# A new order table for a decayed linear attention and a feed-forward layer on one core

## The chip, the core and the metric

The kernel runs on one core of a Trainium2 chip. A core has TensorE (PE; its weight loads are shown as PEld), VectorE (DVE), ScalarE (ACT), GpSimd (POOL) and SyncE (SP), which here only issues transfers, and sixteen DMA engines that all queues share. The metric is device time of one launch in microseconds (us). Before the change it is 187.21 us, the median of three runs (187.03 to 187.23). Profiles come from one further execution of the same program.

## The reference

There are 4 batches, 8 heads, 768 steps and 48 channels a head. First a recurrence with a complex decay, then a layer norm and a feed-forward layer with a residual:

```python
mag = np.sqrt(a_re * a_re + a_im * a_im)
scale = np.minimum(mag, 0.999) / (mag + 1e-06)
...
for t in range(S):
    new_re = ar * S_re - ai * S_im
    new_im = ar * S_im + ai * S_re
    kv = np.einsum('bhd,bhe->bhde', k[:, :, t], v[:, :, t])
    S_re, S_im = (new_re + kv, new_im)
    y[:, :, t] = np.einsum('bhd,bhde->bhe', q[:, :, t], S_re)
...
xn = (x - mu) / np.sqrt(var + 1e-06) * g_ln
ch = np.maximum(xn @ w_ch1, 0.0) @ w_ch2
return (x + ch).astype(np.float32)
```

The output is 4 x 768 x 384 in float32; w_ch1 is 384 x 1536, w_ch2 is 1536 x 384.

## The kernel before

The 768 steps of a batch are cut into chunks of 128 steps, two chunks make a pair, three pairs a batch; so pairs P run from 0 to 11 and chunks n from 0 to 23, with n = 2P + c. The running product of the decays is replaced by cumulative sums of logarithms and of angles, made by matmuls with triangular matrices.

For a pair: loads of are, aim, k, q, vf (v as float32) on SP; `ln`, `iv`, `th`, `u` on ScalarE and `r`, `r2`, `l`, `lc` on VectorE or GpSimd turn a_re and a_im into log magnitude and angle; `dec` and `ph` are the matmuls that sum these; `e` and `en` are the decay and its inverse, `sin` and `cos` the rotation. The decay products are `ke` = k * en and `qe` = q * e, two halves a pair (`ke.P.0.m`), and `ks`, `qs` multiply these by cos and sin (`.0` is cos, `.1` sin). Pair 0 is worked in two halves of four heads, so there the third part of a name is always one of these halves (`qs.0.0.0`: half 0, cos).

For a chunk: `kT`, `qT` transpose ks and qs on TensorE (line 598), `ksT`, `qsT` copy the result out of PSUM; or, where the table gives `ksT` or `qsT` to SP, a transfer that transposes does both, and kT or qT is left out (line 603). `am` multiplies the two (line 621), `atm` masks, `gm` is the sum of k and v products (line 645) that `G` carries on, `y` the attention's output (lines 682 and 685). `v` is vf as bfloat16 (lines 408 and 410). Then `bn` and `x` for the norm, `xtr` and `xT` the transpose of x (line 719; or a transfer, line 725), `mm1` and `relu` (lines 752, 764, 766), `mm2` (line 776), `ot` (line 791) and the store `st` (line 797). `xr` and `rstd` finish the norm behind the matmuls.

The weights come by two transfers on GpSimd's queue: `wl.0` (line 365) and `wl.1` (line 367). They land as bfloat16. `ngl` (line 373) is the negated norm gain, and `wc` (line 381, VectorE) scales the first weights by it in nine pieces. All of `mm1` needs these.

Nothing is scheduled by a planner at run time. `PLAN` (line 42) is a table in which each word is an operation, its engine (P, A, V, G, S) and, for what uses PSUM, its first bank; a name behind "@" is an operation on another engine after which this one may start ("turns at the shared port"). Each engine runs its words in the order of the table, and waits for what an operation needs, for its tile's buffer (`RINGS`: three of q and k, two of vf, ten of x) and for its bank. SP sends its transfers in order too. `warm` are matmuls on a constant that fill TensorE (lines 806 and 810); `tab` loads ScalarE's function tables (line 815).

Of the kernel before, what the change touches and what calls it, by code (L numbers as in the profile page):

```python
# [846 lines left out]
```

## Time and profile before

| | before |
|---|---|
| median of three runs | 187.21 us |
| the profiled execution, span from first to last instruction | 185.6 us |
| TensorE, VectorE, ScalarE, GpSimd busy | 177.0, 157.7, 154.6, 99.8 us |
| transfers on SP's queue | 127616 packets, 32.65 MB |
| of these, transposes: ksT, qsT, xT | 8, 7, 4 |
| read from and written to device memory | 28.31 MB, 4.72 MB |

The profiled execution is known by its span alone; launch and end lie outside it. A group row of the profile gives line, engine, operation, what is written and read, shape and count, then busy time and the mean duration of one in ns, then the engine's idle time ahead of these instructions and what ended most of it. Matmuls overlap, so their mean duration is longer than the pace at which they follow each other; the pace is read from the chain of waits.

### The profile page before, as it was taken

To read this page: it belongs to the slowest core of one execution; us is meant where nothing else is said; L and a number is where in the kernel's file an instruction comes from. 1 tells how busy PE (TensorE), PEld (TensorE's weight loads), DVE (VectorE), ACT (ScalarE), POOL (GpSimd) and SP (SyncE) were. 2 spreads that over 40 slices of the span, in tenths; PEclk is the share of its full clock that TensorE was granted. 3 is DMA by queue.
4 is the path that set the end of the run, shared out by engine and by line. 5 is a ranking of instruction groups with operands and counts; after the bars stand their busy time and mean duration, and the time that the engine had idled before them with its cause. 6 is when DMAs were issued, how large, how long until landed. Compare 5 with 4: busy or idle time off the path is not lost.

```text
span 185.6 us, 5131 instructions
## 1 busy us (share of the span) xinstructions
PE 177.0 (95%) x2029; PEld 139.0 (75%) x2029; DVE 157.7 (85%) x302; ACT 154.6 (83%) x218; POOL 99.8 (54%) x128
## 2 busy tenths in 40 slices
...
GB/s 154 309 229 206 246 199 191 206 143 189 262 187 213 226 228 230 212 273 181 222 238 151 168 150 241 190 227 200 183 159 139 246 147 202 163 193 73 70 82 87
DMA packets 128440, 35.34 MB, mean 190 GB/s; under 512 B 124448, under 2 KB 127648, under 8 KB 128416
## 3 DMA queue, kind: packets, MB, share of 16 engines
q1 hardware_dynamic: 127616, 32.65, 81.4%
q0 software_dynamic: 800, 2.36, 7.2%
...
HBM read 28.31 MB, written 4.72 MB: 178 GB/s over the span
## 4 chain that ended last, share of the span: by engine, by line
PE 59%; ACT 14%; DMA 10%; DVE 10%; issue 3%; SPq 2%; DVEq 0%
PE banks L752 22%; PE banks L776 19%; DMA w1b<-in_moe_w_ch_dram 7%; PE banks L598 4%; PE banks L621 4%; ACT L815 3%; PE banks L484 2%; DMA are<-in_a_re_dram 2%; DMA k<-in_k_dram 2%; ACT are L457 2%; PE banks L682 2%; DVE l L473 1%; ACT h L764 1%; PE banks L685 1%; ACT w L455 1%
## 5 line engine op out<-in xcount | busy, mean ns | idle before, releaser
L752 PE MATMUL banks<-xT,w1b 128*128 128x256 bf16 x432 | 52.7, 273 | 0.2
L776 PE MATMUL banks<-w2b,h 128*128 128x384 bf16 (+2 forms) x300 | 52.5, 319 | 0.0
L752 PEld LDWEIGHTS <-w1b 128*128 128x128 bf16 x432 | 45.8, 114 | 1.7 <-DVE w1b L381 0.4
L764 ACT ACTIVATE h<-banks 128x1024 bf16<-128x1024 f32 x33 | 32.8, 1022 | 8.3 <-PE banks L752 8.1
L776 PEld LDWEIGHTS <-h 128*128 128x128 bf16 x300 | 26.9, 97 | 14.1
L292 DVE TENSOR_TENSOR atm<-banks,mask 128x1024 bf16<-128x1024 f32 x24 | 28.9, 1218 | 1.9 <-PE banks L621 1.6
L815 ACT ACT_TABLE_LOAD x15 | 19.2, 1283 | 1.0 <-PEq L831 0.8
L292 POOL TENSOR_TENSOR ke<-k,en 128x384 bf16<-128x384 f32 x14 | 12.7, 916 | 8.3 <-DVE l L476 5.6
L292 POOL TENSOR_TENSOR qe<-q,e 128x384 bf16<-128x384 f32 x15 | 13.7, 916 | 6.1 <-DVE w1b L381 1.9
L292 POOL TENSOR_TENSOR ks<-ke,trig 128x768 bf16<-128x768 bf16 x7 | 11.4, 1643 | 6.4 <-PE banks L752 4.2
L621 PE MATMUL banks<-qsT,ksT 128*128 128x128 bf16 x192 | 14.6, 219 | 0.1
L410 POOL TENSOR_SCALAR v<-vf 128x768 bf16<-128x768 f32 x7 | 5.8, 831 | 16.0 <-DVE r L292 8.9
L810 PE MATMUL banks<-u_e 128*128 128x512 f16 x42 | 11.7, 418 | 2.2 <-POOL u_e L320 2.2
L292 POOL TENSOR_TENSOR r<-aim,are 128x768 f16<-128x768 f32 x7 | 12.7, 1817 | 1.9 <-ACT x L699 1.5
L709 POOL TENSOR_SCALAR xr<-x,mv 128x384 f32<-128x384 bf16 x16 | 9.3, 586 | 8.1 <-PE banks L752 3.3
L621 PEld LDWEIGHTS <-ksT 128*128 128x128 bf16 x192 | 12.0, 98 | 1.8 <-DVE ksT L289 0.5
L692 DVE BATCH_NORM_STATS2 stats<-banks 128x6 f32<-128x384 f32 x24 | 13.4, 556 | 0.1
L682 PE MATMUL banks<-v,atm 128*128 128x48 bf16 x192 | 12.1, 183 | 0.3 <-ACT x L699 0.2
L473 DVE SCALAR_TENSOR_TENSOR l<-r,w 128x768 f16<-128x768 f16 (+1 forms) x13 | 11.5, 892 | 0.9 <-ACT r L469 0.7
L791 DVE SCALAR_TENSOR_TENSOR ot<-banks,rstd,xr 128x384 f32<-128x384 f32 (+2 forms) x18 | 10.5, 590 | 2.0 <-PE banks L776 1.6
L455 ACT ACTIVATE w<-are 128x768 f32<-128x768 f32 (+1 forms) x13 | 10.2, 790 | 2.3 <-DMA are<-in_a_re_dram 2.3
L682 PEld LDWEIGHTS <-atm 128*128 128x128 bf16 x192 | 11.0, 96 | 1.2 <-DVE atm L292 0.2
...
## 6 DMA issues: line engine op xcount, KB each, us to landing
k<-in_k_dram SPq DMA_DIRECT2D x24, 192.0 KB, 4.1
q<-in_q_dram SPq DMA_DIRECT2D x24, 192.0 KB, 4.2
vf<-in_v_dram SPq DMA_DIRECT2D x24, 192.0 KB, 4.0
out_dram<-ot SPq DMA_DIRECT2D x23, 192.0 KB, 3.4
are<-in_a_re_dram SPq DMA_DIRECT2D x8, 384.0 KB, 4.7
aim<-in_a_im_dram SPq DMA_DIRECT2D x8, 384.0 KB, 4.8
are<-in_a_re_dram SPq DMA_DIRECT2D x8, 192.0 KB, 3.7
aim<-in_a_im_dram SPq DMA_DIRECT2D x8, 192.0 KB, 3.8
```

The lines of the kernel that those rows point to most:

```text
L292: {"DVE": nc.vector, "POOL": nc.gpsimd}[eng(name)].tensor_tensor(**kw)
L455: add(f"ln.{X}", lambda S_=S_: act(out=S_("w"), in_=S_("are"), func=AF.Ln), needs=[f"are.{X}"], uses=[("are", P), ("w", P)])
L473: nc.vector.scalar_tensor_tensor(out=S_("l"), in0=S_("r2"), scalar=0.5, in1=S_("w"), op0=ALU.mult, op1=ALU.add)
L621: nc.tensor.matmul(ps[:, h], lhsT=T("ksT", n)[:, h], rhs=T("qsT", n)[:, h], start=True, stop=True)
L682: nc.tensor.matmul(ps[:, h], lhsT=T("atm", n)[:, h], rhs=T("v", P)[:, c, h], start=True, stop=nfirst)
L692: nc.vector.bn_stats(out=T("stats", n), in_=bank(f"y.{n}")[:, 0:DM])
L752: nc.tensor.matmul(ps[:, jj], lhsT=w1b[:, dc, ts(gi, JG * C)].rearrange("k (p j) -> k j p", j=JG)[:, jj], rhs=T("xT", P)[:, dc].rearrange( ...
L764: act(out=dst, in_=src, func=AF.Relu)
L776: nc.tensor.matmul(bank(f"o.{N}")[:, ws], lhsT=T("h", P)[:, j, ts(c, C)], rhs=w2b[:, j, ws], start=(j == 0), stop=(j == NJ - 1))
L791: nc.vector.scalar_tensor_tensor(out=o, in0=bank(f"o.{N}")[:, ws], scalar=T("rstd", P)[:, ds(c, 1)], in1=xs, op0=ALU.mult, op1=ALU.add)
L810: g.add(f"warm.w{i}", lambda i=i: nc.tensor.matmul(bank(f"warm.w{i}"), lhsT=u_e[:, 0, 0], rhs=u_e.rearrange("p c j t -> p (c j t)"), start ...
L815: g.add(f"tab.{nm}.{i}", lambda tab=tab: nc.scalar.preload_act_table_set(tab))
```

## The change

Only the table is new. It holds the same operations but for the transposes that go from TensorE to the transfer queue, and one evacuation.

- Eight more transposes are transfers: qsT.11, ksT.13, qsT.14, ksT.16, qsT.19, qsT.21 (six of ks or qs), xT.10 and xT.23. With them kT.13, kT.16, qT.11, qT.14, qT.19, qT.21, xtr.10 and xtr.23 leave TensorE.
- From VectorE to GpSimd: ten of the half products ke and qe in balance (GpSimd 14 and 15 before, 19 and 20 after), two r, two r2, two v, one G; in balance one ks, one qs, one xr and one ot go the other way.
- Between ScalarE and VectorE: x is 9 on ScalarE and 15 on VectorE before, 16 and 8 after; relu 33 and 3 before, 29 and 7 after; abs 6 and 2 before, 3 and 5 after.
- The order changes on all engines, the first loads included. On GpSimd the words between wl.0 and wl.1 were ke.1.0.0, ke.1.0.1, ks.1.0.1, ks.1.0.0, one, r.3.0, v.1, xr.0, ngl, r2.3.0; now they are ke.1.0.1, v.0, ke.1.0.0, ks.1.0.0, r.3.0, v.1, r2.3.0, one, ke.2.0.0, ngl.

The start of the table, up to the first mm1, before and after, and from the rest the lines with a new transposing transfer:

```diff
@@ -40,105 +40,104 @@
-are.1.0:S ue:G are.0.0:S are.0.1:S pad.qs.1:G pad.ks.2:G aim.1.0:S ident:G car0.0:G pad.qs.2:G aim.0.0:S tab.log.0:A
-ln.1.0:A uec:G aim.0.1:S qrow:G iv.1.0:A uth:V are.2.0:S zdec:G@uth ln.0.0:A car0.1:G@uth ln.0.1:A pick:G@uth iv.0.1:A
-k.0.0:S pad.qs.0:G iv.0.0:A q.0.1:S r.1.0:V q.0.0:S r.0.1:V tab.trig.1:A th.1.0:A r.0.0:V r2.0.1:V th.0.1:A r2.1.0:V
-vf.0.1:S th.0.0:A r2.0.0:V warm.w0:P0 warm.w1:P0 warm.w2:P0 warm.w3:P0 warm.w4:P0 warm.w5:P0 warm.w6:P0 warm.w7:P0
-warm.w8:P0 warm.w9:P0 warm.w10:P0 warm.w11:P0 warm.w12:P0 warm.w13:P0 warm.w14:P0 warm.w15:P0 warm.w16:P0 warm.w17:P0
-warm.w18:P0 warm.w19:P0 warm.w20:P0 warm.w21:P0 warm.w22:P0 warm.w23:P0 warm.w24:P0 warm.0:P0 warm.1:P0 warm.2:P0
-ph.0.1:P0 pad.ks.0:G@r2.0.0 aim.2.0:S ph.0.0:P6 car.0.1:V0 mask:G@r2.0.0 car.0.0:V6 pad.ks.1:G@r2.0.0 k.0.1:S
-warm.w25:P1 warm.3:P1 warm.4:P1 ph.1.0:P2 tab.log.2:A u.0.1:A u.0.0:A l.0.1:V k.1.1:S u.1.0:A l.0.0:V lc.0.1:V
-ln.2.0:A car.1.0:V2 q.1.1:S warm.w26:P1 warm.w27:P1 warm.5:P1 warm.6:P1 dec.0.1:P1 lc.0.0:V l.1.0:V en.0.1:A1
-warm.7:P4 dec.0.0:P7 e.0.1:A1 iv.2.0:A q.1.0:S lc.1.0:V qe.0.1.0:V warm.w28:P4 warm.w29:P4 warm.8:P4 warm.9:P4
-warm.10:P4 dec.1.0:P4 en.0.0:A7 uthc:V vf.0.0:S e.0.0:A7 r.2.0:V e.1.0:A4 warm.11:P1 warm.12:P1 dps.0:P7 are.3.0:S
-r2.2.0:V en.1.0:A4 ke.0.0.0:V u.2.0:A gln:S ke.0.1.0:V qe.0.0.0:V aim.3.0:S qe.1.0.1:V qe.1.0.0:V k.1.0:S l.2.0:V
-tab.trig.3:A sin.0.0:A6 sin.0.1:A0 warm.w30:P1 warm.w31:P1 warm.w32:P1 warm.w33:P1 warm.13:P1 warm.14:P1@en.1.0
-warm.w34:P1 warm.w35:P1 warm.w36:P1 warm.w37:P1 warm.15:P1 warm.16:P1@qe.0.0.0 warm.w38:P1 warm.w39:P1 warm.w40:P1
-warm.17:P1 warm.18:P1 warm.19:P1 warm.20:P1 qt.0.0:P6 qs.0.0.1:V sin.1.0:A2 qt.0.1:P0 ks.0.0.1:V vf.1.1:S lc.2.0:V
-cos.0.0:A6 ks.0.1.1:V warm.21:P1 warm.22:P1 qt.1.0:P2 qs.1.0.1:V cos.0.1:A0 vf.1.0:S dps.1:P5 qs.0.1.1:V cos.1.0:A2
-dec.2.0:P0 ks.0.1.0:V k.2.1:S ks.0.0.0:V decc.0:A7 qs.0.1.0:V kT.0:P6 decc.1:A5 qs.0.0.0:V th.2.0:A qs.1.0.0:V
-wl.0:G@qs.0.0.0 qT.0:P2 q.2.1:S v.0:V qT.1:P3 ksT.0:A6 qsT.0:V2 qT.2:P4 ke.1.0.0:G@v.0 k.2.0:S kT.1:P5 qsT.1:A3
-qsT.2:V4 am.0:P6 ke.1.0.1:G@v.0 ksT.1:V5 gm.0:P4 atm.0:V6 ks.1.0.1:G warm.23:P2 warm.24:P2 am.1:P2 qT.3:P5 tab.log.4:A
-ln.3.0:A atm.1:V2 y.0:P6 ks.1.0.0:G G.0:A4 e.2.0:A0 warm.w41:P7 warm.25:P7 warm.26:P7 warm.27:P7 gm.1:P4 bn.0:V6
-ph.2.0:P2 iv.3.0:A qsT.3:V5 one:G kT.2:P7 x.0:A6 G.1:V4 r.3.0:G en.2.0:A0 ksT.2:V7 warm.28:P5 xtr.0:P6 kT.3:P4 xT.0:V6
-am.2:P0 ksT.3:V4 y.1:P5 v.1:G atm.2:V0 am.3:P6 tab.trig.5:A th.3.0:A xr.0:G gm.2:P4 bn.1:V5 ngl:G sin.2.0:A2 r2.3.0:G
-ph.3.0:P0 atm.3:V6 x.1:A5 q.2.0:S car.3.0:A0 y.2:P5 G.2:V4 sin.3.0:A0 xtr.1:P7 qt.2.0:P2 are.4.0:S wc.1.1:V gm.3:P4
-xT.1:A7 wc.1.0:V qt.3.0:P0 wc.1.2:V cos.2.0:A2 wl.1:G@xT.1 vf.2.0:S wc.0.0:V mm1.0.1.0:P6 wc.0.1:V cos.3.0:A0 bn.2:V5
+ue:G are.0.1:S are.1.0:S are.0.0:S uth:V aim.1.0:S warm.13:P5 pad.qs.1:G warm.w5:P5 warm.w40:P5 aim.0.0:S ident:G
+warm.w17:P1 warm.7:P3 warm.0:P4 warm.w41:P2 aim.0.1:S uec:G warm.27:P3 tab.log.0:A ln.0.1:A warm.w24:P0 warm.w29:P2
+pick:G@uth are.2.0:S warm.w33:P4 iv.0.1:A warm.w25:P7 warm.6:P1 warm.w13:P3 warm.w22:P6 ln.1.0:A car0.1:G@uth
+warm.w14:P5 qrow:G warm.w11:P5 gln:S warm.18:P2 warm.w23:P1 ln.0.0:A zdec:G@uth q.0.1:S car0.0:G warm.w15:P6 iv.1.0:A
+warm.24:P3 warm.w3:P5 warm.25:P1 warm.8:P2 warm.26:P0 q.1.0:S warm.w19:P1 iv.0.0:A warm.20:P5 r.1.0:V warm.w27:P7
+warm.w16:P6 warm.w4:P1 warm.w26:P2 warm.w31:P7 k.0.0:S r.0.0:V warm.w10:P1 warm.w39:P5 r2.0.0:V warm.22:P1
+tab.trig.1:A th.1.0:A warm.10:P6 warm.12:P5 r.0.1:V warm.w21:P5 warm.w6:P7 k.0.1:S warm.w20:P4 th.0.0:A r2.0.1:V
+warm.4:P5 warm.w0:P2 th.0.1:A r2.1.0:G warm.5:P4 q.0.0:S ph.0.1:P1 warm.16:P4 warm.9:P4 aim.2.0:S ph.0.0:P0 car.0.1:V1
+pad.ks.0:G@r2.0.0 tab.log.2:A u.0.1:A warm.w8:P4 pad.qs.0:G warm.w30:P7 q.1.1:S u.0.0:A warm.w9:P6 l.0.1:V
+mask:G@r2.0.0 warm.w2:P4 u.1.0:A warm.11:P6 l.0.0:V pad.ks.1:G@r2.0.0 vf.0.1:S lc.0.1:V ln.2.0:A l.1.0:V dec.0.1:P4
+k.2.0:S en.0.1:A4 lc.0.0:V iv.2.0:A lc.1.0:V dec.0.0:P6 ke.0.1.0:V dec.1.0:P2 aim.3.0:S e.0.0:A6 car.0.0:V0 e.0.1:A4
+r.2.0:V k.1.0:S e.1.0:A2 warm.w7:P4 qe.0.1.0:V en.0.0:A6 vf.1.0:S r2.2.0:V en.1.0:A2 warm.w34:P6 ke.0.0.0:V are.3.0:S
+u.2.0:A qe.1.0.0:V ph.1.0:P2 qe.1.0.1:V l.2.0:V vf.0.0:S warm.w12:P6 dps.0:P7 warm.w35:P6 warm.14:P6@en.1.0 decc.0:V7
+k.1.1:S qe.0.0.0:G tab.trig.3:A sin.0.0:A0 car.1.0:V2 sin.0.1:A1 qt.0.0:P0 sin.1.0:A2 q.2.1:S qt.0.1:P1 lc.2.0:V
+ks.0.0.1:V qs.0.1.1:V cos.0.0:A0 qt.1.0:P2 qs.0.0.1:V cos.0.1:A1 ks.0.0.0:V vf.1.1:S warm.w18:P6 warm.28:P4 ks.0.1.1:V
+th.2.0:A warm.15:P6 warm.w28:P4 qs.0.0.0:V warm.w38:P6 qs.0.1.0:V q.2.0:S wl.0:G@qs.0.0.0 cos.1.0:A2 ks.0.1.0:V
+qT.0:P6 qs.1.0.1:V warm.19:P5 are.4.0:S warm.17:P1 qs.1.0.0:V kT.0:P4 qsT.0:V6 kT.1:P2 ke.1.0.1:G k.2.1:S qT.3:P0
+ksT.0:V4 tab.log.4:A ln.3.0:A qT.1:P5 v.0:G@qsT.0 ksT.1:V2 warm.3:P1 am.0:P6 qsT.1:A5 qsT.3:V0 ke.1.0.0:G qT.2:P3
+dps.1:P2 atm.0:V6 iv.3.0:A warm.21:P1 warm.w1:P4 ks.1.0.0:G@qsT.3 am.1:P0 decc.1:A2 warm.w36:P5 aim.4.0:S qsT.2:A3
+atm.1:V0 warm.2:P2 gm.0:P2 dec.2.0:P4 G.0:A2 ks.1.0.1:V en.2.0:A4 y.0:P0 gm.1:P2 uthc:V bn.0:V0 kT.2:P3 r.3.0:G@uthc
+e.2.0:A4 kT.3:P6 ksT.2:V3 x.0:A0 y.1:P4 G.1:V2 xtr.0:P5 am.2:P0 ksT.3:V6 v.1:G warm.w37:P2 ph.2.0:P2 atm.2:V0 r2.3.0:G
+tab.trig.5:A th.3.0:A am.3:P6 xT.0:A5 bn.1:V4 ph.3.0:P0 sin.2.0:A2 one:G ke.2.0.0:G atm.3:V6 vf.2.0:S x.1:A4 y.2:P5
+ngl:G@bn.1 sin.3.0:A0 wl.1:G wc.1.2:V xtr.1:P7 wc.1.1:V qt.2.0:P2 car.3.0:A0 wc.1.0:V gm.2:P4 xT.1:A7 q.4.1:S
+pad.ks.2:G wc.0.0:V qt.3.0:P0 G.2:V4 cos.2.0:A2 qe.2.0.0:G warm.1:P6 mm1.0.1.0:P6 bn.2:V5 vf.2.1:S cos.3.0:A0
...
...
+qsT.11:S G.8:V7 dec.6.0:P4 car.6.0:A0 abs.6.0:V0 k.5.0:S am.8:P2 r2.7.0:G e.6.0:A4 vf.5.0:S mm2.6.0:P6 atm.8:V2
...
+mm2.9.1:P1 x.10:A0 qe.6.0.1:G gm.10:P2 iv.9.0:A ph.8.0:P4 G.10:V2 xT.10:S qs.6.0.0:V mm2.8.0:P2 ks.6.0.1:V y.11:P3
+qs.6.0.1:V ksT.13:S mm2.9.2:P1 tab.trig.11:A sin.8.0:A4 bn.11:V3 r.9.0:G@qs.6.0.1 kT.12:P7 abs.8.0:A4 x.11:V3
...
+en.8.0:A2 qsT.14:S y.12:P6 mm2.10.1:P1 r.10.0:G bn.12:V6 x.13:A4 mm2.10.2:P1 e.8.0:A2 qsT.15:S x.12:V6 xtr.13:P7
...
+qs.8.0.0:V en.10.0:A6 ksT.16:S mm2.12.0:P3 ot.13:V1 qs.8.0.1:G@ks.8.0.0 bn.15:V0 mm2.12.1:P3 st.13:S xtr.14:P2 x.15:V0
...
+ke.9.0.0:V gm.16:P2 qsT.18:S y.16:P3 G.16:V2 relu.7.1:A0 ks.9.0.1:G ph.11.0:P4 bn.16:V3 qsT.19:S am.17:P6 cos.10.0:A
...
+G.19:V7 x.19:A5 xT.18:S mm2.16.0:P6 qs.10.0.0:V en.11.0:A2 qs.10.0.1:V mm2.16.1:P6 e.11.0:A2 xr.17:V qsT.21:S
...
+xr.19:G mm1.10.2.1:P4 xT.22:S ot.19:G@x.22 mm2.20.1:P6 relu.10.2:A4 mm2.21.0:P2 xT.23:S mm2.20.2:P6 mm2.21.1:P2
...
```

141 lines of the change are left out of this document (66 added, 75 removed).

## The prediction

> **What bounds the kernel now.** I read the page's first part, then the busy time by stretches, cut where the first matmul of the expert layer (mm1.0, line 752) starts and at later stage borders. The columns are PE, PEld, DVE, ACT, POOL busy, granted clock, DMA share, GB/s.
>
> ```profile
> span 185.6 us, 5131 instructions
> PE 177.0 (95%) x2029; PEld 139.0 (75%) x2029; DVE 157.7 (85%) x302; ACT 154.6 (83%) x218; POOL 99.8 (54%) x128
> 0.00:37.48 37.48, 32.63 (x317) 20.01 (x318) 28.70 (x58) 33.90 (x53) 18.74 (x40) 1.00 0.99 216
> 37.48:104.48 67.00, 66.96 (x796) 54.73 (x797) 63.88 (x125) 64.95 (x89) 37.45 (x41) 1.00 0.98 209
> 104.48:130.86 26.38, 26.27 (x324) 21.48 (x321) 24.94 (x49) 25.23 (x36) 17.53 (x19) 1.00 0.97 202
> 130.86:164.71 33.85, 33.82 (x425) 28.22 (x422) 29.65 (x58) 25.46 (x37) 20.64 (x22) 1.00 0.90 173
> 164.71:182.02 17.31, 17.30 (x178) 14.55 (x175) 10.13 (x16) 5.04 (x6) 5.40 (x9) 1.00 0.33 94
> ```
>
> From 37.48 us to 182.02 us TensorE is never idle (144.4 of 144.5 us) at full clock. ScalarE and VectorE stand just below it until 104 us (64.95 and 63.88 of 67.00), and the DMA engines are filled until 131 us. So the time has three terms: the start of mm1.0, the TensorE work behind it, and 3.6 us of last output and store behind 182.02. The first two are what this change touches.
>
> The chain of waits (start, length, what) gives TensorE's pace and what stood ahead of mm1.0:
>
> ```profile
> 24.53 12.18 DMA w1b<-in_moe_w_ch_dram
> 37.48 0.89 PE banks L752 x6
> 46.53 0.89 PE banks L598 x16
> 74.69 0.33 PE banks L719 x6
> 143.22 0.20 PE banks L645 x8
> ```
>
> The first expert weights are asked for at 24.53 and land 12.18 us later. Eight transposes of line 598 take 0.445 us, three of line 719 take 0.17, a G product of line 645 takes 0.20.
>
> **TensorE's work.** Six groups of eight transposes (kT.13, kT.16, qT.11, qT.14, qT.19, qT.21) and two of three (xtr.10, xtr.23) leave TensorE, all of them behind mm1.0: 6 x 0.445 + 2 x 0.17 = 3.0 us. Against this gm.3 (0.20) and two filler matmuls move from ahead of mm1.0 to behind it.
>
> ```profile
> L810 PE MATMUL banks<-u_e 128*128 128x512 f16 x42 | 11.7, 418 | 2.2 <-POOL u_e L320 2.2
> L806 PE MATMUL banks<-u_e 128*128 128x256 f16 x29 | 5.5, 273 | 0.0
> ```
>
> Fillers cost 11.7/42 = 0.28 and 5.5/29 = 0.19, so 0.67 comes back; I take 0.7. Net behind mm1.0: -2.3 us. Where TensorE has no idle time, this is time, if the other engines can keep pace.
>
> **VectorE, ScalarE, GpSimd.** Ten decay products (ke, qe) go from VectorE to GpSimd.
>
> ```profile
> L292 POOL TENSOR_TENSOR ke<-k,en 128x384 bf16<-128x384 f32 x14 | 12.7, 916 | 8.3 <-DVE l L476 5.6
> L292 DVE TENSOR_TENSOR ke<-k,en 128x384 bf16<-128x384 f32 x10 | 5.4, 549 | 0.0
> L292 POOL TENSOR_TENSOR r<-aim,are 128x768 f16<-128x768 f32 x7 | 12.7, 1817 | 1.9 <-ACT x L699 1.5
> L289 DVE COPY qsT<-banks 128x1024 bf16<-128x1024 bf16 x16 | 10.8, 682 | 1.1 <-PE banks L598 1.0
> ```
>
> That is +9.2 us for GpSimd (10 x 0.916) and -5.5 for VectorE. GpSimd also gets two r (3.6) and some smaller operations, and would be near 99.8 + 14 = 114 us of some 183: no bound by its sum. VectorE loses six copies of transposed tiles (6 x 0.68 = 4.1), seven x go to ScalarE, four relu and three abs come back from it; by the groups' mean durations VectorE ends about 9 us lower and ScalarE about 4 lower. Both stay under TensorE, so the 2.3 us should hold.
>
> **The start.** In the new table the weights' request wl.0 still waits for qs.0.0.0 (line 365's queue is POOL's), but r2.1.0, uthc, qe.0.0.0, qs.1.0.1, ks.0.1.0 and qs.0.1.0 no longer stand ahead of that on VectorE. ScalarE then sets it: qs.0.0.0 needs cos.0.0. (The rows: landing times of the page's part 6, ScalarE's timeline, VectorE's piece of the chain and its timeline.)
>
> ```profile
> are<-in_a_re_dram SPq DMA_DIRECT2D x8, 384.0 KB, 4.7
> are<-in_a_re_dram SPq DMA_DIRECT2D x8, 192.0 KB, 3.7
> 19.21 1.28 ACT L815 ACT_TABLE_LOAD   x1
> 21.96 1.60 ACT L532 ACTIVATE trig<-banks 128x384 bf16<-128x384 int16 x3
> 24.86 0.99 ACT L287 COPY ksT<-banks 128x1024 bf16<-128x1024 bf16 x1
> 23.39 0.69 ACT L287 COPY dec<-banks 48x8 f32<-48x8 f32 x4
> 36.68 0.47 ACT L287 COPY xT<-banks 128x384 bf16<-128x384 bf16 x1
> 23.86 0.67 DVE qs L292 x2
> 36.81 1.58 DVE L381 TENSOR_SCALAR w1b<-w1b,ngl 128x512 bf16<-128x512 bf16 x5 [0.46 <-DMA w1b<-in_moe_w_ch_dram]
> ```
>
> A half tile of are is now loaded first, and lands up to 1.0 us sooner (4.7 against 3.7); ScalarE then waits for the whole one behind it, so I take 0.5 of that. ScalarE's order up to its table load at 19.21 has the same operations, so the load comes at 18.7; cos.0.0 (first of the group at 21.96, 0.5 long) ends near 22.0, three VectorE products of 0.3 follow, and wl.0 goes out near 23.2: 1.3 us sooner. It lands near 35.4, and the scaling of line 381 (0.7 from 36.81 until mm1.0 could start) ends near 36.1. But the weights are not the only thing that mm1.0 waits for: it needs xT.1, which ScalarE finished at 37.15, 0.3 ahead of mm1.0. On ScalarE's way there ksT.0 (1.0) and decc.0 (0.3) leave, and qsT.2 (1.0) and xT.0 (0.5) come: xT.1 ends near 36.8, and mm1.0 starts near 37.0. Of 1.3 us I count 0.5; the bounds are no gain (if ScalarE has to wait once more) and 1.3.
>
> **The transfer queue.** Six transposes of 128x1024 bf16 (256 KB) and two of 128x384 (96 KB) are added.
>
> ```profile
> q1 hardware_dynamic: 127616, 32.65, 81.4%
> q0 software_dynamic: 800, 2.36, 7.2%
> ksT<-ks SPq DMA_TRANSPOSE x8, 3.6
> ```
>
> At the queue's mean rate (32.65 MB in 81.4% of 185.6 us, 0.216 MB/us) these are 6 x 1.2 + 2 x 0.45 = 8.1 us of all sixteen engines; 7.7 of it (all but xT.23) is needed before 164.7 us. The stretches leave open 0.4 + 1.3 + 0.8 + 3.4 = 5.9 us there. The missing 1.8 can come out of the lead with which loads land ahead of their use, or late loads stall something. One transposed tile lands 3.6 us behind its issue, where copies took 0.68, so am.n for these tiles may also come later. I charge 0.6 us, nearer to the lower end, since the loads were rarely waited for; the ends are 0 and 1.8.
>
> **Sum.** 185.6 - 0.5 (start) - 2.3 (TensorE) + 0.6 (transfers) = 183.4 us of span. The median of the runs, 187.21, stands 1.6 over the profiled span, so 185.0 us. Own range 183.4 (start 1.3 sooner, transfers at nothing, fillers at 0.5) to 186.7 (start at nothing, transfers at 1.8).
>
> **First rival: the load behind the weights (slower).** v.1 on GpSimd needs both halves of vf.1. In the old table these were the 22nd and 23rd requests of SP; now vf.1.1 is the 25th, and the request for the weights goes out sooner. What SP has in flight when a weight transfer begins is held up:
>
> ```profile
> DMA to landing us min/median/max: 3.4/5.1/8.7
> DMA to landing us min/median/max: 3.5/4.2/12.1
> 25.56 1.80 POOL L292 TENSOR_TENSOR ke<-k,en 128x384 bf16<-128x384 f32 x2
> 32.61 0.83 POOL L410 TENSOR_SCALAR v<-vf 128x768 bf16<-128x768 f32 x1
> 33.98 0.25 POOL L373 TENSOR_SCALAR ngl<-gln 128x3 f32<-128x3 f32 x1
> 34.22 1.46 POOL L292 TENSOR_TENSOR r<-r 128x768 f16<-128x768 f16 x1
> 30.61 0.10 POOL L315 MEMSET half_n<- 128x2 f32 x1
> ```
>
> The first two rows are the loads of k between 15 and 45 us and of vf up to 60 us: the longest, 8.7 and 12.1 us, were those caught by the two weight transfers. [...] If vf.1.1 is caught as the second load in line, it lands near the weights' end, 35.7. And ngl, which the scaling waits for, now stands behind it on GpSimd: v.1 0.83, r2.3.0 1.46, half_n 0.1, ke.2.0.0 0.92, ngl 0.25 make 39.2, and 0.7 later mm1.0 starts at 39.9 instead of 37.0: 185.0 + 2.9 = 187.9 us. It decides once vf.1.1 lands after about 32.7 us. For it: the place in the queue. Against it: caught as first in line it lands near 32, as k did, and costs nothing.
>
> **Second rival: the transfers become the bound (slower).** If loads have no lead to give, the 1.8 us that don't fit push the last transposes (needed by am.22 and am.23) later than before, TensorE waits for them, and what it saves is lost in those waits: 187.2 + 1.8 = 189.0 us. It decides once the transfers lag the old table's by more than the loads' lead. For it: a DMA share of 0.97 to 0.99 until 131 us. Against it: 3.4 us are open between 131 and 165 us, where most new transposes stand.
>
> **Third rival: GpSimd and VectorE at each other's cost.** [...] If some four of the added operations each hold VectorE up by a product's 0.55 us once TensorE has run dry, 2.2 us are lost: 187.2, no change. [...] Against it: VectorE's 9 us of relief.
>
> **That the change does nothing** is the case where ScalarE, not TensorE, sets the pace up to 104 us. It too is relieved by 4 us; I count it with the third.
>
> **How the numbers follow.** Forecast 0.52, first rival 0.22, second 0.13, third 0.13. A difference under 0.2% (186.84 to 187.58) can't be told from none. Faster: nearly all of the forecast, a third of the third rival and a quarter of the first, where only part of its price is paid: 0.51 + 0.04 + 0.06 = 0.61. Slower: the second, two thirds of the first and a little of the third: 0.13 + 0.15 + 0.02 = 0.30. Same: 0.09. The range 183.4 to 188.8 leaves out the forecast's lower tail and most of the second rival.
>
> **What would show it.** Right: wl.0 issued near 23.2, mm1.0 (first line 752) near 37.0, TensorE busy without a gap from there to about 179.8, and 264 matmuls in line 598 become 216. First rival: v on POOL starts after 33, ngl ends near 39, VectorE idle ahead of line 381. Second: waits of PE, ACT or POOL that end by DMA k, vf, ksT or qsT, beyond 100 us. Third: VectorE products longer than 0.55 or idle ahead of them, PE gaps that end by DVE. The prediction is wrong as a whole if TensorE shows over 3 us of idle time behind mm1.0.

## The result and the profile after

The changed kernel takes 206.25 us (median of four runs, 204.56 to 207.32) where the old one took 187.12 beside it: a ratio of 1.099 (95% interval 1.095 to 1.104), slower by 19 us. 185.0 was forecast. The profiled execution's span is 204.8 us, 19.2 over the old one's 185.6. One execution of each run was profiled; for a_rstd and a_banks it was the slowest of four (204.3 and 209.0 us), for e_tile_full the fastest (186.9), and the ratios below leave out executions over 1.5% above their run's fastest.

The page of the changed kernel, its busy times and the granted clock in 40 slices:

```profile
span 204.8 us, 5067 instructions
...
PE 181.3 (89%) x1975; PEld 139.2 (68%) x1975; DVE 164.3 (80%) x283; ACT 158.1 (77%) x217; POOL 120.3 (59%) x143
...
PEclk9999889969999999999999996999999999999999
...
q1 hardware_dynamic: 134784, 34.42, 82.3%
```

TensorE ran 54 matmuls less, and was busy 4.3 us longer: four of the forty slices show a clock under 0.9, where the old page had none. The busy time by stretches, cut at the first mm1.0 as for the old kernel (columns as before):

```profile
0.00:41.02 41.02, 33.69 (x308) 21.52 (x308) 31.00 (x57) 35.25 (x53) 22.89 (x42) 0.96 1.00 213
41.02:201.20 160.18, 147.16 (x1663) 117.42 (x1664) 132.68 (x226) 122.85 (x165) 97.41 (x101) 0.98 0.88 174
```

mm1.0 starts at 41.02 instead of 37.48. Behind it TensorE was idle for 0.2 us before, now for 13.0 (160.18 less 147.16). To separate work from waiting I gave each TensorE operation behind mm1.0 its pace in the old trace (from its start to the next one's): the sum is the work, and what lies beyond it is waiting or half clock. Work fell from 144.6 to 142.1 us, waiting rose from -0.1 to 18.5. So 3.5 (start) - 2.5 + 18.6 and 0.4 less behind the last matmul make the 19.2. The waiting comes from four kinds of places.

**VectorE held up by GpSimd.** VectorE's and GpSimd's timelines of the changed kernel (start, length):

```profile
59.78 1.97 DVE L475 TENSOR_SCALAR l<-l 128x768 f16<-128x768 f16 x1
```
```profile
59.72 1.81 POOL L291 TENSOR_TENSOR r<-aim,are 128x768 f16<-128x768 f32 x1 [0.40 <-ACT are L456]
```

lc.4.0 should last 0.35 us. It starts 0.06 us behind r.5.0 on GpSimd and ends 0.2 us behind its end; dec.4.0 needs it, and TensorE is idle from 60.57 to 61.80. VectorE's groups, shapes apart (busy, mean ns of one), first of the old kernel, then of the new:

```profile
L292 DVE TENSOR_TENSOR ks<-ke,trig 128x768 bf16<-128x768 bf16 x15 | 8.3, 554 | 0.0
...
L476 DVE TENSOR_SCALAR l<-l 128x768 f16<-128x768 f16 x11 | 3.9, 354 | 0.1
...
L709 DVE TENSOR_SCALAR xr<-x,mv 128x384 f32<-128x384 bf16 x8 | 3.3, 413 | 0.0
...
L381 DVE TENSOR_SCALAR w1b<-w1b,ngl 128x512 bf16<-128x512 bf16 x9 | 2.7, 365 | 0.5 <-DMA w1b<-in_moe_w_ch_dram 0.5
```
```profile
L291 DVE TENSOR_TENSOR ks<-ke,trig 128x768 bf16<-128x768 bf16 x16 | 10.6, 681 | 0.3 <-POOL ke L291 0.2
...
L708 DVE TENSOR_SCALAR xr<-x,mv 128x384 f32<-128x384 bf16 x9 | 6.9, 773 | 0.0
...
L475 DVE TENSOR_SCALAR l<-l 128x768 f16<-128x768 f16 x11 | 6.1, 566 | 0.1
...
L380 DVE TENSOR_SCALAR w1b<-w1b,ngl 128x512 bf16<-128x512 bf16 x9 | 4.3, 531 | 0.0
```

The same operations last longer: 773 ns against 413, 566 against 354. Over all VectorE instructions that last more than 15% and 0.1 us beyond the usual time of their operation and shape, this excess is 0.6 us in the old trace and 14.2 in the new one; nearly every one of them lies beside a GpSimd instruction and ends 0.1 to 0.8 us after it. So this waiting shows as a long busy instruction (1.97 us instead of 0.35), not as idle time.

**Function tables.** ScalarE's timeline of the changed kernel:

```profile
144.40 1.28 ACT L734 ACT_TABLE_LOAD   x1
145.70 0.20 ACT L734 ACTIVATE rstd<-mv 128x2 f32<-128x2 f32 x1
145.92 1.28 ACT L735 ACT_TABLE_LOAD   x1
...
147.94 1.28 ACT L491 ACT_TABLE_LOAD   x1
149.24 0.84 ACT L491 ACTIVATE th<-r 128x768 f16<-128x768 f16 x1
```

In the new table rstd.7 is on ScalarE between sin.10.0 and th.11.0. A load of 1.28 us stands ahead of each of its two functions, another ahead of th.11.0 and a fourth at 153.70, at the lines of these functions themselves: 5.1 us. In the old trace all fifteen loads are at line 815, none at the lines of its four rstd on ScalarE. TensorE is idle from 145.95 (2.02 us) and from 150.10 (1.80 us), waiting for banks that ScalarE has not read.

**Half clock.** The stretches around TensorE's longest idle time (it ends by sin.9.0):

```profile
118.90:122.00 3.10, 0.18 (x7) 0.17 (x4) 3.10 (x4) 1.39 (x3) 2.06 (x4) 1.00 0.98 251
122.92:126.34 3.42, 3.42 (x27) 2.01 (x26) 1.89 (x3) 3.16 (x5) 0.57 (x1) 0.50 1.04 206
```

Three stretches of 3.41 us ran at half clock: from 23.94, 41.0 and 122.92, which lie 5 and 24 such lengths apart. In the 3.41 us ahead of each, TensorE had been idle for part of the time (busy for 1.55, 2.36 and 0.98 us). Its busy share there does not decide alone:

```profile
37.59:41.00 3.41, 2.36 (x34) 1.31 (x32) 3.41 (x5) 3.36 (x7) 2.95 (x5) 1.00 0.98 143
41.00:44.41 3.41, 3.39 (x29) 2.61 (x30) 1.84 (x6) 1.41 (x3) 0.00 (x0) 0.50 0.95 169
...
150.23:153.64 3.41, 1.74 (x35) 1.41 (x35) 1.21 (x3) 3.39 (x4) 1.73 (x2) 1.00 1.10 212
```

Busy for 2.36 of 3.41 us was followed by half clock, busy for 1.74 (until 153.64) was not.

**Tiles that come late.** mm1.5, mm1.9, am.21 and am.22 wait 0.43 + 0.72 + 0.66 + 0.40 = 2.2 us for xT.10, xT.18, qsT.21 and qsT.22, which the transfer queue transposes; xT.10 and qsT.21 are new there.

### The profile page after: what moved, and what is told of

Same layout as the page of the kernel before. It is cut to its first block, busy times and chain, and to the rows that moved or that the text cites. A ratio compares the mean times of both kernels' runs of the same rounds, so it can differ in the third digit from the quotient of the medians.

```text
span 204.8 us, 5067 instructions
## 1 busy us (share of the span) xinstructions
PE 181.3 (89%) x1975; PEld 139.2 (68%) x1975; DVE 164.3 (80%) x283; ACT 158.1 (77%) x217; POOL 120.3 (59%) x143
## 3 DMA queue, kind: packets, MB, share of 16 engines
q1 hardware_dynamic: 134784, 34.42, 82.3%
q0 software_dynamic: 800, 2.36, 6.6%
## 4 chain that ended last, share of the span: by engine, by line
PE 44%; DVE 21%; ACT 11%; DMA 11%; issue 5%; POOL 4%; SPq 3%; POOLq 0%; DVEq 0%; ACTq 0%
PE banks L751 12%; PE banks L775 12%; PE banks L809 5%; DMA qsT<-qs 4%; PE banks L597 3%; PE banks L620 3%; DMA aim<-in_a_im_dram 2%; DVE atm L291 2%; DVE l L472 2%; PE banks L483 2%; ACT h L763 2%; DVE ks L291 2%; PE banks L805 2%; DVE stats L691 2%; ACT trig L520 2%
## 5 line engine op out<-in xcount | busy, mean ns | idle before, releaser
L751 PE MATMUL banks<-xT,w1b 128*128 128x256 bf16 x432 | 54.5, 277 | 4.3 <-ACT car L512 2.0
L775 PE MATMUL banks<-w2b,h 128*128 128x384 bf16 (+2 forms) x300 | 54.4, 322 | 0.0
L763 ACT ACTIVATE h<-banks 128x1024 bf16<-128x1024 f32 x29 | 29.1, 1020 | 13.9 <-PE banks L751 9.2
L291 POOL TENSOR_TENSOR qe<-q,e 128x384 bf16<-128x384 f32 x20 | 20.2, 1014 | 16.0 <-DVE xT L288 7.1
L291 POOL TENSOR_TENSOR r<-aim,are 128x768 f16<-128x768 f32 x9 | 16.6, 1840 | 15.1 <-ACT h L763 6.3
L291 POOL TENSOR_TENSOR ke<-k,en 128x384 bf16<-128x384 f32 x19 | 17.5, 923 | 9.6 <-DVE sh L539 6.1
L814 ACT ACT_TABLE_LOAD x15 | 19.2, 1283 | 1.0 <-PEq L830 0.8
L809 PE MATMUL banks<-u_e 128*128 128x512 f16 x42 | 14.8, 446 | 1.1 <-ACT en L487 0.7
L472 DVE SCALAR_TENSOR_TENSOR l<-r,w 128x768 f16<-128x768 f16 (+1 forms) x13 | 13.2, 1024 | 0.1
L409 POOL TENSOR_SCALAR v<-vf 128x768 bf16<-128x768 f32 x9 | 7.5, 834 | 8.8 <-DMA vf<-in_v_dram 5.4
L291 POOL TENSOR_TENSOR ks<-ke,trig 128x768 bf16<-128x768 bf16 x6 | 10.2, 1702 | 3.9 <-DVE ke L291 2.7
L291 DVE TENSOR_TENSOR ks<-ke,trig 128x768 bf16<-128x768 bf16 (+1 forms) x20 | 11.9, 616 | 0.4 <-POOL ke L291 0.2
```

The lines of the kernel that those rows point to most:

```text
L291: {"DVE": nc.vector, "POOL": nc.gpsimd}[eng(name)].tensor_tensor(**kw)
L472: nc.vector.scalar_tensor_tensor(out=S_("l"), in0=S_("r2"), scalar=0.5, in1=S_("w"), op0=ALU.mult, op1=ALU.add)
L751: nc.tensor.matmul(ps[:, jj], lhsT=w1b[:, dc, ts(gi, JG * C)].rearrange("k (p j) -> k j p", j=JG)[:, jj], rhs=T("xT", P)[:, dc].rearrange( ...
L763: act(out=dst, in_=src, func=AF.Relu)
L775: nc.tensor.matmul(bank(f"o.{N}")[:, ws], lhsT=T("h", P)[:, j, ts(c, C)], rhs=w2b[:, j, ws], start=(j == 0), stop=(j == NJ - 1))
L809: g.add(f"warm.w{i}", lambda i=i: nc.tensor.matmul(bank(f"warm.w{i}"), lhsT=u_e[:, 0, 0], rhs=u_e.rearrange("p c j t -> p (c j t)"), start ...
```

## The experiments

Each run changes words of one of the two tables (a_fill and e_all also add ten fillers, e_sp_line adds loads, f_stores and f_stores_tiles change the engine in the line that stores); the diffs show the core of it. In the table, "ratio" is to the old kernel run on the same chip. Start of mm1.0, work and waiting (as above) and VectorE's excess are from each run's profile, in us.

| run | median us | ratio (95%) | mm1.0 | work | waiting | VectorE's excess |
|---|---|---|---|---|---|---|
| old table | 187.1 | | 37.5 | 144.6 | -0.1 | 0.6 |
| new table | 206.3 | 1.099 (1.095-1.104) | 41.0 | 142.1 | 18.5 | 14.2 |
| a_rstd | 202.1 | 1.076 (1.071-1.082) | 41.6 | 142.1 | 15.7 | 15.8 |
| a_turns | 200.2 | 1.069 (1.065-1.072) | 39.9 | 142.1 | 13.1 | 5.4 |
| a_tr | 209.2 | 1.116 (1.112-1.120) | 40.8 | 145.2 | 17.4 | 12.2 |
| a_st | 206.5 | 1.104 (1.100-1.108) | 42.4 | 142.1 | 16.0 | 14.2 |
| a_banks | 206.1 | 1.096 (1.088-1.104) | 42.3 | 142.1 | 19.7 | 13.3 |
| a_fill | 204.5 | 1.089 (1.083-1.095) | 39.4 | 142.1 | 19.2 | 14.0 |
| b_turns_rstd | 198.1 | 1.055 (1.050-1.060) | 39.1 | 142.1 | 10.6 | 5.9 |
| b_turns_rstd_store | 197.3 | 1.052 (1.047-1.057) | 39.7 | 142.1 | 11.8 | 5.3 |
| b_turns_rstd_back | 197.5 | 1.054 (1.049-1.058) | 39.8 | 145.2 | 7.3 | 5.0 |
| e_all | 195.3 | 1.037 (1.031-1.043) | 38.2 | 145.2 | 5.7 | 2.5 |
| c_no_fillers | 189.8 | 1.012 (1.008-1.016) | 39.6 | 144.6 | 0.7 | 0.4 |
| d_transposes | 191.8 | 1.023 (1.017-1.028) | 37.3 | 142.0 | 8.1 | 1.3 |
| d_no_turns | 201.7 | 1.076 (1.071-1.081) | 37.4 | 144.6 | 14.7 | 16.5 |
| e_sp_line | 192.6 | 1.026 (1.021-1.031) | 37.4 | 144.6 | 4.2 | 0.4 |
| e_tile_room | 188.0 | 1.002 (0.999-1.004) | 37.4 | 144.2 | 1.2 | 0.4 |
| e_tile_full | 188.1 | 1.002 (0.999-1.004) | 37.4 | 144.2 | 0.1 | 0.4 |
| f_stores_tiles | 192.9 | 1.025 (1.017-1.033) | 37.4 | 142.0 | 6.9 | 3.0 |
| f_stores | 187.8 | 0.998 (0.994-1.001) | 37.4 | 144.6 | 2.1 | 1.2 |

### The new table, one cause taken away at a time

a_rstd:

```diff
-abs.10.0:V6 am.16:P4 rstd.7:A G.15:G
+abs.10.0:V6 am.16:P4 rstd.7:G G.15:G
```

> One word of the new table: rstd.7 from ScalarE back to GpSimd. Theory L (the loss is a sum of separate local waits: VectorE instructions held up by GpSimd's, four more function-table loads of 1.28 us around rstd.7, a start 3.5 us later, half clock after idle stretches of TensorE): the four loads at 144.40, 145.92, 147.94 and 153.70 go, with them TensorE's idle stretches at 145.95 (2.02 us) and 150.10 (1.80 us); 206.2 - 3.8 = 202.4 us, 201.5 to 203.5. Rival T (the transfers became the bound, so that time saved at one place comes back as a later wait for a load or a transposed tile): 205 to 206.5.

Measured: 202.1 us, in the range of theory L, and the two idle stretches shrink to one of 0.51. The four loads cost 4.2 us.

a_turns (four of the twelve; where needed, the word moves behind the one it waits for):

```diff
-r2.1.0:G   qe.0.0.0:G        r.5.0:G        ks.7.0.0:G
+r2.1.0:G@r2.0.1 qe.0.0.0:G@l.2.0 r.5.0:G@lc.4.0 ks.7.0.0:G@ks.7.0.1
```

> The new table with every operation on its engine, but twelve GpSimd operations that run beside a lengthened VectorE instruction get a turn behind it (r2.1.0, qe.0.0.0, wl.1, G.3, r.5.0, r.8.0, ke.7.0.0, ks.7.0.0, ke.8.0.0, qe.10.0.1, ke.10.0.0, qe.11.0.1). Theory L: VectorE's lengthened instructions (14.2 us in the new trace) shrink to under 5 us; the scaling ahead of mm1.0 gives back 1.7 us, TensorE's idle stretches at 60.57 (1.23 us) and 119.02 (2.92 us, and the half clock behind it, 1.7 us) go: 206.2 - 7.5 = 198.7 us, 197.5 to 201. Rival T: 204.5 to 206.5, since the loads and tiles come no sooner. A third view (the lengthened instruction is only where the waiting is booked, the work of the two engines must go one after the other anyway): GpSimd is later by what VectorE gains, 204 to 207.

Measured: 200.2 us, 6.0 sooner and in the range of theory L, with the same operations in the same order on every engine. VectorE's and GpSimd's timelines of this run, at the place shown above:

```profile
57.21 0.36 DVE L474 TENSOR_SCALAR l<-l 128x768 f16<-128x768 f16 x1
```
```profile
57.71 1.83 POOL L290 TENSOR_TENSOR r<-aim,are 128x768 f16<-128x768 f32 x1 [0.94 <-DVE l L474]
```

GpSimd waits 0.9 us, VectorE's instruction lasts 0.36 instead of 1.97, and TensorE's stretch is gone. The excess fell to 5.4, where under 5 was expected. That the waiting is only booked elsewhere (204 to 207 us) is ruled out: it matters which of the two engines waits.

a_tr: kT.13, kT.16, qT.11, qT.14, qT.19, qT.21, xtr.10, xtr.23 on TensorE again, and their copies, for instance:

```diff
-ksT.16:S
+kT.16:P7 ... ksT.16:V7
```

> The new table with the eight transposes back on TensorE and eight evacuations back (seven on VectorE, xT.10 on ScalarE). Rival T: the backlog of the transfer queue goes; under 200 us. Theory L: TensorE gets back 3.0 us of work, and TensorE's idle stretches that end by a transposed tile go (113.01, 171.44, 173.86, 182.97: 0.43 + 0.72 + 0.66 + 0.40 = 2.2 us): 205.5 to 208 us.

Measured: 209.2, slower still, a us beyond the upper end of theory L. Rival T (under 200 us) is ruled out. TensorE's work rose by 3.1 us and its waiting fell by 1.1. Eight copies came back to VectorE and ScalarE, and am.13 waits 3.4 us instead of 2.9; that the copies make this wait longer is not shown.

a_st:

```diff
-q.3.1:S st.0:S vf.3.1:S st.1:S vf.3.0:S q.4.0:S aim.6.0:S
+q.3.1:S vf.3.1:S vf.3.0:S q.4.0:S aim.6.0:S st.0:S st.1:S
```

> The new table with four loads (vf.3.1, vf.3.0, q.4.0, aim.6.0) moved ahead of st.0 in SP's order, so that the line does not stand still from 53.6 to 62.3 us until ot.0 is there. Rival S (the loads kept back behind the first store set the pace from 60 to 115 us): aim.6.0 lands near 60 instead of 69.9, r.6.0 and v.3 start sooner, 202 to 204 us. Theory L: v.3 has a turn behind lc.5.0 and stays where it is; 205.3 to 206.5 us.

Measured: 206.5, no gain. SP's longest wait (8.7 us) cost nothing. mm1.0 starts at 42.4 here although nothing ahead of it was changed: in the new table and the runs whose edits lie behind mm1.0 (a_rstd, a_tr, a_st, a_banks) it starts anywhere from 40.8 to 42.4.

a_banks:

```diff
-abs.9.0:V0 car.9.0:A0 am.12:P2 sin.9.0:A0
+car.9.0:A0 sin.9.0:A0 abs.9.0:V0 am.12:P2
```

> The new table with car.9.0 and sin.9.0 (ScalarE) ahead of abs.9.0 (VectorE); all three read the same bank. If readers of one bank on two engines go one after the other in the table's order: ScalarE no longer waits 3.3 us for VectorE at 117.3, sin.9.0 ends near 118.7, am.13 starts when abs.9.0 is done (120.6 instead of 121.9), TensorE's idle stretch of 2.92 us shrinks to about 1.5, and the half clock behind it may go too: 203 to 205.2 us. If the two readers don't wait for each other: no change, 205.5 to 207.

Measured: 206.1 (204.6 to 209.0), no gain that can be told; the time lies in the range for readers that don't wait. But the mechanism is there. ScalarE's timeline in the new table, and in this run:

```profile
120.58 0.48 ACT L512 ACTIVATE car<-banks 32x384 f16<-32x384 int16 x1 [3.27 <-DVE sh L539]
```
```profile
119.58 0.48 ACT L511 ACTIVATE car<-banks 32x384 f16<-32x384 int16 x1
```

In the new table car.9.0 waited 3.27 us for a VectorE instruction whose result it does not use; it only reads the same bank. With the order turned round it follows relu.5.1 (which ends at 119.56) at once, and am.13's idle stretch falls from 2.92 to 0.67. am.14 then waits 2.05 us for qsT.14, from the transfer queue. mm1.5 waits 1.92 us for xT.10 instead of 0.43, but ahead of the edit, and this wait differs in other runs too (0.36 in b_turns_rstd, 2.58 in a_rstd). Where the saving went stays open.

a_fill: seven fillers moved from behind qt.1.0, and ten more, into TensorE's idle stretches ahead of qt.1.0.

> The new table with seven fillers that stood behind qt.1.0 moved into TensorE's idle stretches between 15 and 23.4 us, and ten more fillers there. If idle time of TensorE brings the half clock at 23.9: clock 1.00 through the start, the first transposes start 1.5 to 3 us sooner, mm1.0 (41.0) near 39: 203 to 205 us. If VectorE and ScalarE alone set the start: mm1.0 within 0.5 us of 41.0, 205.5 to 207 us.

Measured: 204.5. Busy time by stretches, of the new table and of this run:

```profile
15.00:23.90 8.90, 5.08 (x34) 2.47 (x34) 8.61 (x20) 8.13 (x15) 1.64 (x1) 1.00 1.02 222
23.94:27.35 3.41, 3.41 (x21) 2.38 (x21) 2.92 (x8) 3.38 (x5) 1.91 (x2) 0.50 0.96 187
```
```profile
15.00:23.90 8.90, 8.05 (x49) 3.77 (x47) 8.61 (x21) 8.09 (x15) 1.69 (x1) 1.00 1.03 227
23.94:39.30 15.36, 13.45 (x201) 10.37 (x201) 15.22 (x27) 15.22 (x23) 12.62 (x14) 1.00 1.00 196
```

TensorE busy for 5.08 of 8.90 us is followed by half clock, busy for 8.05 it is not, and mm1.0 starts at 39.4, 1.6 us sooner than in the new table and ahead of the 40.8 to 42.4 above. The half clock at mm1.0's start is still there:

```profile
39.33:42.74 3.41, 3.36 (x29) 2.55 (x30) 1.88 (x6) 1.42 (x3) 0.00 (x0) 0.50 1.07 202
```

### The causes together

b_turns_rstd has both edits, a_rstd's and a_turns'.

> The new table with both edits, the twelve turns and rstd.7 on GpSimd. Theory L (separate local waits, whose costs add up): 206.3 - 6.0 - 4.2 = 196.1 us, 195 to 197.5. Rival T, now as the next bound (with the first waits gone, am.n waits for tiles that the transfer queue transposes: 2.03 us at am.14, 0.61 at am.16, 0.60 at mm1.5, 0.41 at am.20 with the turns alone): these waits grow, 198 us or more.

Measured: 198.1, outside theory L's range and at the edge of rival T's; the interval (196.7 to 198.7) reaches into both. 8.2 of 10.2 us add up. The wait at am.14 hardly grew, from 2.03 to 2.15 us; the one at am.21 is 1.33, where the new table had 0.66.

b_turns_rstd_store adds a_st's four loads.

> As the one before, with the four loads ahead of st.0 in SP's order too. If the loads that stood behind the first store make the later backlog of the transfer queue: the waits for transposed tiles from 100 to 140 us shrink by 1.5 us or more, 193.5 to 195 us. If not: within 0.7 us of the one before.

Measured: 197.3; the difference of 0.8 lies within the intervals. The wait at am.14 is 2.34 us, so the early loads are not what fills the queue there.

b_turns_rstd_back adds a_tr's transposes to the two edits instead.

> The twelve turns, rstd.7 on GpSimd, and the eight transposes back on TensorE with their evacuations on VectorE and ScalarE. Rival T: the waits for transposed tiles (3.6 us with the turns alone) go, 3.0 us of TensorE work comes back, and loads come sooner: 193 to 196 us. Theory L without T (VectorE's copies cost as much as without the turns, where undoing the transposes made it 2.9 us slower): 198 to 200 us.

Measured: 197.5, between the two ranges. TensorE's work is 3.1 us more and its waiting 3.3 less: in the new order the eight tiles are worth nothing by either way.

e_all adds a_fill, a_banks and three turns to that:

```diff
-qe.2.0.0:G ks.10.0.0:G@xr.16 ke.9.0.1:G
+qe.2.0.0:G@wc.0.2 ks.10.0.0:G@l.11.0 ke.9.0.1:G@qe.9.0.0
```

> The new table with all waits found so far taken away: the twelve turns, rstd.7 on GpSimd, the eight transposes back on TensorE, the fillers in TensorE's first idle stretches, car.9.0 and sin.9.0 ahead of abs.9.0, and three more turns (qe.2.0.0 behind wc.0.2, ks.10.0.0 behind l.11.0, ke.9.0.1 behind qe.9.0.0). Theory L: 197.5 (turns, rstd.7 and transposes undone) less 1.8 for the start and 1 to 3 for the rest: 193.5 us, 192 to 195.5; behind mm1.0 TensorE's work is 145 us and its waits shrink from 7.3 to 5 us or less. If something else than these waits makes the new table slow: 196.5 to 198.

Measured: 195.3, at the upper end of the range. By the profile (span 192.3): start 38.2, work 145.2, waiting 5.7, and 3.3 behind it. No single large loss is left, but 195.3 is still 7.7 us over the old table's 187.6 in the same series. The new order has ten places of 0.3 to 0.8 us left, and what makes each of them stays open. No version of it that I ran beats the old table.

### The old table, one part at a time

c_no_fillers leaves nineteen filler matmuls out, which add nothing to the result:

```diff
-dps.0:P7 ... warm.w30:P1 warm.w31:P1 ... warm.19:P1 warm.20:P1 qt.0.0:P6
+dps.0:P7 ... qt.0.0:P6
```

> The old table without the nineteen filler matmuls between dps.0 and qt.0.0 (17.4 to 21.0 us). If idle time of TensorE brings the half clock: the profile shows about 3.5 us without matmuls there and then a stretch of 3.4 us at clock 0.5, in which the first transposes run; mm1.0 starts 1 to 2 us later, 188.3 to 189.5 us. If the clock goes by something else: clock 1.00 throughout, 187.1 to 187.6 us.

Measured: 189.8, 0.3 beyond the range, with half clock for twice the time expected. Its stretches:

```profile
17.40:21.00 3.60, 0.00 (x0) 0.00 (x1) 3.56 (x8) 3.57 (x6) 0.00 (x0) 1.00 0.94 197
...
21.45:28.28 6.83, 6.83 (x52) 4.83 (x52) 4.36 (x13) 5.30 (x11) 3.67 (x4) 0.50 1.06 213
```

3.6 us without matmuls bring 6.8 us at clock 0.50, and mm1.0 comes 2.1 us later. 6.83 us is twice the 3.41 us that each stretch at half clock lasts in the new table; what sets this length is not shown. TensorE need not be idle for as long as 3.6 us: in the new table, ahead of 23.94, it was busy for 5.08 of 8.90 us and never idle for more than 1.05.

d_transposes: six of the eight new transposes (without xT.10 and xT.23), at places in SP's line that I chose.

```diff
-kT.16:P3 ksT.16:V3
+ksT.16:S
```

> The old table with one part of the change alone: qsT.11, ksT.13, qsT.14, ksT.16, qsT.19, qsT.21 as transfers that transpose, kT.13, kT.16, qT.11, qT.14, qT.19, qT.21 and their copies left out. If the term of the prediction holds (TensorE's work is time, 6 x 0.445): 187.3 - 2.7 = 184.6 us, 184.2 to 186. Rival T (transfers the bound, late tiles): 187 to 189.5 us, with idle TensorE ahead of am.n of these chunks or with loads late.

Measured: 191.8, 4.4 us slower and beyond both ranges. TensorE's work fell by 2.6 us, where 2.7 were costed, and 8.1 us of waiting came. The largest wait, in TensorE's timeline, then SP's timeline and the queue's row of this run:

```profile
135.92 0.62 PE L619 MATMUL banks<-qsT,ksT 128*128 128x128 bf16 x8 [2.88 <-DMA ksT<-ks]
```
```profile
130.52 0.79 SPq L795 DMA_DIRECT2D out_dram<-ot  x1
131.35 0.44 SPq L398 DMA_DIRECT2D q<-in_q_dram  x1
131.90 1.69 SPq L601 DMA_TRANSPOSE ksT<-ks  x1
133.64 0.58 SPq L398 DMA_DIRECT2D k<-in_k_dram  x1
```
```profile
q1 hardware_dynamic: 133952, 34.22, 87.1%
```

SP issues without a pause, each tile holds it 1.23 us or more where the shortest loads take 0.37, and the line is 4.4 us behind the old one just ahead of ksT.16 (the load of q goes out at 131.35 instead of 126.91). The packets' time rose from 81.4% of 185.6 to 87.1% of 190.7, by 15.0 us: 2.5 us of all engines a tile, not 1.2. (Runs that move the old table's bytes differ by up to 5 us among themselves, from 75.2% of 200.1 in d_no_turns to 79.4% of 195.6 in b_turns_rstd_back. In the old trace the 256-byte packets that the transposes alone have took 24 ns each, which is 1.5 us a tile; in this run they took 27 on average, the old tiles' included.)

d_no_turns takes forty names behind "@" out and changes nothing else, for instance:

```diff
-ke.1.0.0:G@v.0
+ke.1.0.0:G
```

> The old table without forty of its turns between GpSimd and VectorE (those at the two weight transfers, at uth and at the fillers stay). Theory L (a VectorE instruction that runs beside certain GpSimd instructions lasts until these are done, and this reaches TensorE): VectorE's lengthened instructions go from 0.6 us to over 5 us, 189 to 194 us. Rival: the waiting is only booked elsewhere, 187 to 187.7 us.

Measured: 201.7, 14 us slower and far beyond theory L's range, and the excess is 16.5: three quarters of what the whole change cost, with the same operations on the same engines. One place of it, VectorE and GpSimd (ks should last 0.55):

```profile
64.94 2.07 DVE L288 TENSOR_TENSOR ks<-ke,trig 128x768 bf16<-128x768 bf16 x1
```
```profile
64.78 1.81 POOL L288 TENSOR_TENSOR r<-aim,are 128x768 f16<-128x768 f32 x1 [1.74 <-DMA aim<-in_a_im_dram]
```

In both pairs shown (lc.4.0 of the new table, ks here) VectorE's instruction starts 0.06 and 0.16 us behind GpSimd's r, and lasts until that is done and 0.2 and 0.4 us longer.

e_sp_line adds loads whose data nothing uses, three at each of six places:

```diff
-k.9.0:S
+nil.9:S nil.10:S nil.11:S k.9.0:S
```

> The old table, all its transposes where they were, with three loads of 1.5 KB (3 words a partition) put into SP's line at each of the six places where the transposes alone went in. They cost SP's time to issue and next to no time of the DMA engines. If SP's line is what made the six transposes cost 4.4 us (they hold SP for 1.23 us or more each, where a load can take 0.4): 188.5 to 191 us. If it was the time of the DMA engines or the way of the tiles themselves: 187.2 to 188 us.

Measured: 192.6, 5.0 us slower, beyond the range for SP's line. SP's timeline at ksT.16's place:

```profile
131.08 1.62 SPq L372 DMA_DIRECT2D nil<-in_moe_g_ln_dram  x3
```

So a longer line of SP is enough to make this kernel slower, with 27 KB moved in all. The packets' time rose too, by 2.7 us (81.3% of 189.2), which is no more than it differs between runs that move the same bytes.

e_tile_room and e_tile_full make one tile each a transfer:

```diff
-qT.19:P1 ... qsT.19:V1
+qsT.19:S
```

> The old table with one tile alone, qsT.19, as a transfer that transposes, put ahead of xT.16, where SP stood idle for 2.3 us before (135.4 to 137.7) and the DMA share is 0.81. If TensorE's work is time where the queue has room: 187.4 - 0.45 = 186.95, 186.6 to 187.2 us. If the tile's cost on the queue outweighs it even here: 187.4 to 188.2 us.

> The old table with one other tile alone, qsT.14, as a transfer ahead of qsT.15, in the stretch from 103 to 135 us where SP issues without a pause and the DMA share is 0.97. If the queue is the bound there: 187.6 to 188.8 us, am.14 or a later tile waits. If TensorE's work is time here too: 186.6 to 187.2 us.

Measured: 188.0 and 188.1 against 187.6, both ratios 1.002 (0.999 to 1.004): the gain (a ratio of 0.998) is ruled out, a loss is not shown. The place made no difference. Whether six tiles together cost more than six times one, the intervals don't tell.

f_stores_tiles and f_stores:

```diff
-add(f"st.{N}", lambda n=n, ws=ws, c=c: nc.sync.dma_start(
+add(f"st.{N}", lambda n=n, ws=ws, c=c: (nc.gpsimd if 4 <= n <= 13 else nc.sync).dma_start(
```

> The old table with the six transposes as transfers (the run that took 191.8 us alone), and the ten stores st.4 to st.13 issued by GpSimd instead of SP, at the same places of the table, where their ot is done. That frees some 6 to 8 us of SP's line where the six tiles need 6 x 1.23 = 7.4; the DMA engines move the same bytes. If SP's line made the tiles late: ksT.16 is issued near 127 instead of 131.9, 186 to 189.5 us. If the engines' time did: 191 to 193 us. GpSimd's ten requests of about 1 us each may cost something of their own; the other run of this call shows that.

> The old table with the ten stores st.4 to st.13 issued by GpSimd and nothing else. If GpSimd has room and VectorE is not held up: 186.8 to 187.8 us. If GpSimd's requests hold VectorE or its own products up: 188 to 190 us.

Measured: 192.9 with the tiles, in the range for the engines' time and no better than without the relief, and no change for the stores alone. (With the stores' requests on GpSimd VectorE's excess is 3.0 us instead of 1.3 with the tiles, and 1.2 instead of the old table's 0.6 without them.) SP's timeline with the tiles:

```profile
128.33 2.27 SPq L398 DMA_DIRECT2D q<-in_q_dram  x1
130.70 1.47 SPq L601 DMA_TRANSPOSE ksT<-ks  x1
```

ksT.16 goes out 1.2 us sooner, not 5: SP's other issues have grown (2.27 us for a load that took 0.44 above). What makes them grow is not shown. Which of the two, SP's line or the engines' time, comes first stays open; the runs show that a tile costs both (1.23 us or more, and 2.5).

## Why the prediction was wrong

**TensorE's term** ("Net behind mm1.0: -2.3 us") was right as work: 264 matmuls in line 598 became 216, and the work measured -2.5. The step that failed is the next sentence: "Where TensorE has no idle time, this is time, if the other engines can keep pace". They kept pace in the old order with a few per cent to spare (64.95 and 63.88 of 67.00 us until 104), and the new order brought 18.5 us of waiting. The prediction's own sign of being wrong as a whole, over 3 us of idle TensorE behind mm1.0, came with 13.0.

**VectorE, ScalarE, GpSimd** ("no bound by its sum", "Both stay under TensorE, so the 2.3 us should hold"): this is the step that cost most. I added up durations of instructions that had never met. As sums of undisturbed instructions they came close: VectorE's 164.3 us less 14.2 of excess is 150.1 (148.7 forecast), ScalarE's 158.1 less 5.1 of table loads is 153.0 (150.6), GpSimd has 120.3 (114). What failed is that the durations would stay. The third rival named what then happened, with four holds of 0.55 us; number and length were estimates that no run shows, there were some twenty, 14.2 us in all. It expected them of products; about half of the held instructions have one tensor as input (lc, xr, wc). A held instruction lasts until GpSimd's is done (lc 1.97 us beside r's 1.81, xr 1.02 beside a product's 0.91), not as long as it does alone (0.35, 0.41), and twelve turns against this are worth 6.0 us (a_turns). The 51 names behind "@" of the new table were read as protection. Of the twelve GpSimd operations that a_turns mends, seven had no name and five had one that let them start too early.

**Four table loads** were in no step at all. The list of moves ahead of the prediction leaves rstd out: rstd.1 and rstd.7 went to ScalarE, three others to GpSimd. The words rstd.7:A and tab stood in the new table, and rstd's two functions in its lines: this could have been read. 4.2 us (a_rstd).

**The start** ("wl.0 issued near 23.2", and mm1.0 at 37.0): wl.0 went out at 25.00. I counted what no longer stood ahead of it and took the other instructions at their old length. With r2.1.0 and qe.0.0.0 on GpSimd, r2.0.0 and qe.0.1.0 on VectorE last 1.50 and 1.26 us; ScalarE's table load comes at 20.14 instead of 18.7. Then 3.41 us at clock 0.50, behind a TensorE that was busy for 5.08 of 8.90 us. The weights landed at 34.99 all the same, 10.0 us behind their request and before the 35.4 forecast, but the scaling of line 381 did not begin then: VectorE was busy with atm and bn until 38.4. VectorE and GpSimd of the changed kernel:

```profile
38.37 2.86 DVE L380 TENSOR_SCALAR w1b<-w1b,ngl 128x512 bf16<-128x512 bf16 x4
```
```profile
38.08 0.25 POOL L372 TENSOR_SCALAR ngl<-gln 128x3 f32<-128x3 f32 x1
38.28 0.83 POOL L366 DMA_DIRECT2D w2b<-in_moe_w_ch_dram  x1
39.12 0.55 POOL L360 MEMSET ks<- 128x512 bf16 x1
39.65 0.90 POOL L291 TENSOR_TENSOR qe<-q,e 128x384 bf16<-128x384 f32 x1
```

Four pieces took 2.86 us beside these, where the old table's five took 1.58. From the scaling's start to mm1.0 it is 2.65 us instead of 0.67: of the 3.5 us by which mm1.0 is late, 1.6 lie ahead of the scaling and 2.0 in it. Of the fillers I asked what they cost, not what they keep: taking nineteen away costs 2.4 us (c_no_fillers).

**The transfers' term** (0.6, bounds 0 and 1.8) was the second rival's ground, and mis-sized. A transposed tile was priced by its bytes at the queue's mean rate, 1.2 us; it measured 2.5 of the engines and 1.23 or more of SP's line, for which I had counted nothing. Eight tiles raised the packets' time by 17.5 us (82.3% of 204.8 against 151.1) where I had 8.1 and 5.9 open. Nor is 1 less the DMA share the room that is left: rows above show shares of 1.02 to 1.10. In the old order six of the tiles make the kernel 4.4 us slower, not 2.1 faster: the second rival, at a larger price than its 1.8.

**The first rival's** cause did not happen: vf.1.1 landed at 27.57. (What it feared had a case in the old trace: q, asked for at 25.02 as the second load beside the weights, landed 12.2 us later, 0.5 behind them.) Two of its signs came by another way. v.1 started at 34.94, behind r.3.0, which had its turn behind uthc at 33.16; and ngl, behind these, ended at 38.33, as VectorE came free. So a VectorE that was done sooner would have waited for ngl.

The gains of the single edits don't add up (8.2 of 10.2 us in b_turns_rstd), and with all of them taken together (e_all) 7.7 of the 19 us are left. That a wait taken away uncovers the next fits these runs, but is not shown wait by wait.
